# The second layer's feed-forward as one part of 448 columns, with other cuts of the kept V and of w2

## The chip, the cores and the metric

The kernel runs on one core of a Trainium2 chip. The metric is the device time of one execution in microseconds. Three runs of the kernel before gave 707.36, 707.47 and 707.51; their median is 707.47. One execution more was recorded by the hardware profiler.

## The reference

Two identical layers of a decoder are applied to four tokens (one for each of four batch rows), x of shape [4, 512]. Each layer is attention over a cache, and then a gated feed-forward, each behind a layer normalisation and added to x:

```
x = x + attention(norm(x), k_cache, v_cache, wq, wo)
x = x + feed_forward(norm(x), w1, w3, w2)

attention:    q = x @ wq                          # 32 heads of 128; 8 key/value heads, 4 query heads each
              p = softmax(q k^T / sqrt(128))      # over 4096 cached positions
              out = (p v) @ wo
feed_forward: h = silu(x @ w1) * (x @ w3)         # 512 -> 1792
              out = h @ w2                        # 1792 -> 512
```

Both layers use the same weights and the same caches. All is f32: the K cache and the V cache hold 67 MB each, wq and wo 8.4 MB each, w1, w3 and w2 3.7 MB each.

## The kernel before, in words

The kernel is a stream of loads into one large buffer, the arena, with 216 places of 256 f32 columns on all 128 partitions (`KB = 256`). One such unit is 131 kB. A list, `plan`, names all loads in the order in which they are issued, all on SyncE's queue; `pump` issues the next load as soon as the arena has a free stretch for it, and `done` gives a load's places back when the last of its parts has been used. Nothing is scheduled by the framework: every engine works in the order of the code.

For each of the eight key/value heads a K load and a V load of 64 units each come in turn. `scores` multiplies the padded q with K into `s_ps` (32 products of 512 columns), `factors` and `exponents` make the softmax, `turn_p` transposes it, and `weigh` multiplies it with V into `o_ps`: two halves of 16 products, each followed by a scaling (on ScalarE for the first, VectorE for the second half), then four transposes. Layer 1 goes through the heads upward, layer 2 downward, so that the last V of layer 1 (head 7, `TURN`) is kept in the arena at places 128 to 191 for layer 2. It is the line `cache("v", 0, TURN, (32, 16, 8, 8))`: four loads of 32, 16, 8 and 8 units, where one tile of V (four products) takes 8 units. Behind it in the plan stand wo, and layer 1's w1, w3 and w2 in small loads.

`project_o` multiplies with wo, `collect` sums the partial rows of x and gives the normalised input, and `feed_forward` does the rest of the layer. In it the 1792 columns are spread over four groups of 32 PSUM partitions, so each group holds 448 columns (`FJ`). They are handled in two parts, 256 (`FA`) and 192 (`FB`) columns: `product` does 16 matmuls of w1 into `s_ps` (four blocks of the 512 inputs, four groups), the same for w3 into `o_ps`; `gate` is a sigmoid on ScalarE and a multiply on VectorE; `join` multiplies with the w3 side. w1 and w3 lie in memory as first all columns of part a, then all of part b, so that each part is one stretch. In layer 2 the loads are w1a and w3a (16 units each), w1b and w3b (12 units each), and w2 in five (8, 8, 8, 2, 2).

`tiles` copies the transposed h to `hT`; `tail_tiles` transposes what lies beyond column 256. In layer 2 w2's 14 row blocks are then multiplied into `x_ps` (four products of 128 columns each), on top of the residual `xt`, which four products with the identity put there. `busy(n)` issues n matmuls whose result nobody reads. At the end `x_ps` is copied and stored.

## Time and profile before

| what | value |
|---|---|
| median of 3 runs | 707.47 us (707.36 to 707.51) |
| the profiled execution | 707.43 us, its span 705.5 us |
| granted TensorE clock, mean | 0.804 of full speed |
| TensorE busy (matmul) | 397.1 us, 56% of the span |
| VectorE, ScalarE busy | 85.0 us, 38.3 us |
| read from memory | 298.85 MB, 424 GB/s over the span |
| share of the load queue in 16 DMA engines' span | 99.1% |
| loads issued by SyncE into the arena | 93 |

The page's busy shares say which engine is full; its queue lines say the same for the DMA engines. A timeline row tells when an engine's instruction began, how long it took, how long the engine stood idle before it, and whose signal ended that idle time. Where that is a DMA, the engine was ahead of the stream; where it is another engine, the stream was ahead. The profile counts each f32 matmul of the program as two records.

### The profile page before, as it was taken

What the parts mean: (1) busy time and instruction counts of PE and PEld (TensorE: products, weight loads), DVE (VectorE), ACT (ScalarE), POOL (GpSimd) and SP (SyncE); (2) the same over time, 40 slices, a digit from 0 to 9 for tenths busy, and PEclk for the clock granted to TensorE, in tenths of its full rate; (3) what the DMA queues carried; (4) which work ended last, traced back from release to release, by engine and by line L of the source; (5) the groups of instructions that cost most, each with busy time, mean ns of one, the idle gap of its engine ahead of it and who ended that gap; (6) DMA issues with size and microseconds to landing.
All of it is one profiled execution on the core that took longest, in us unless ns stands there. A gap on an engine that the chain in (4) does not pass through costs nothing. (4 is left out here: it accounts for less than half of the span.)

```text
span 705.5 us, 6894 instructions
## 1 busy us (share of the span) xinstructions
PE 397.1 (56%) x3082; PEld 132.4 (19%) x3082; DVE 85.0 (12%) x290; ACT 38.3 (5%) x87; POOL 2.9 (0%) x10
## 2 busy tenths in 40 slices
PE   4455453545565553547687894265563645477665
PEld 2112011111111110112143231021110211122224
DVE  2001010101001010101111111011000101010111
ACT  0000000000000000002001000000000000000101
POOL 0000000000000000000000000000000000000000
PEclk9866787767778777779899988777787868689899
DMA  9999999999999999999999999999999999999997
GB/s 387 461 402 472 413 424 439 438 421 427 454 420 436 438 425 435 427 426 421 415 404 390 402 438 445 435 431 425 438 436 431 436 435 425 442 410 433 422 425 289
DMA packets 13716, 299.36 MB, mean 424 GB/s; under 512 B 1655, under 2 KB 1783, under 8 KB 6007
## 3 DMA queue, kind: packets, MB, share of 16 engines
q1 hardware_dynamic: 13552, 298.92, 99.1%
q8 instruction: 24, 0.39, 0.2%
q14 instruction: 5, 0.04, 0.0%
q10 hardware_dynamic: 135, 0.01, 0.0%
HBM read 298.85 MB, written 0.07 MB: 424 GB/s over the span
## 5 line engine op out<-in xcount | busy, mean ns | idle before, releaser
L394 PE MATMUL o_ps<-arena 128*32 128x512 f32 x1024 | 145.4, 716 | 149.5 <-DMA arena<-in_v 135.8
L351 PE MATMUL s_ps<-arena,qpad 128*32 128x512 f32 x1024 | 149.1, 736 | 85.4 <-DMA arena<-in_kt 85.4
L394 PEld LDWEIGHTS o_ps<-arena 128*32 128x32 f32 x1024 | 37.0, 129 | 256.6 <-issue 222.3
L351 PEld LDWEIGHTS s_ps<-arena,qpad 128*32 128x32 f32 x1024 | 39.4, 131 | 178.1 <-issue 162.8
L403 DVE SCALAR_TENSOR_TENSOR p<-o_ps,parts,p 128x512 f32<-128x512 f32 x16 | 12.0, 750 | 269.4 <-PE o_ps L394 269.4
L358 DVE TENSOR_REDUCE top<-s_ps 128x1 f32<-128x512 f32 x16 | 11.0, 690 | 194.5 <-PE s_ps L351 194.5
L295 PE MATMUL o_ps<-arena,xpad 128*32 128x512 f32 x112 | 15.5, 680 | 11.6 <-DMA arena<-in_wq 11.6
L401 ACT ACTIVATE p<-o_ps,parts 128x512 f32<-128x512 f32 x16 | 11.0, 687 | 191.9 <-PE o_ps L394 183.5
L425 PE MATMUL x_ps<-arena,oT 128*4 128x512 f32 x104 | 15.2, 702 | 9.3 <-DMA arena<-in_wo 5.8
L382 PE MATMUL t_ps<-ident,p 128*128 128x128 f32 x64 | 11.4, 304 | 13.5 <-ACT p L376 13.5
L405 PE MATMUL t_ps<-ident,p 128*128 128x128 f32 x64 | 10.5, 287 | 14.3 <-DVE p L403 14.2
L369 ACT ACTIVATE f<-d 128x1 f32<-128x1 f32 x16 | 3.2, 203 | 257.2 <-DVE d L367 257.2
L376 ACT ACTIVATE p<-s_ps,top 128x512 f32<-128x512 f32 x16 | 10.9, 684 | 76.9 <-PE t_ps L405 76.9
L383 DVE COPY arena<-t_ps 128x512 f32<-128x512 f32 x16 | 11.1, 691 | 9.7 <-PE t_ps L382 9.7
L405 PEld LDWEIGHTS t_ps<-ident,p 128*128 128x128 f32 x64 | 6.7, 141 | 28.8 <-DVE p L403 28.8
L239 PE MATMUL m_ps<-ident,rows 128*32 128x128 f32 x70 | 11.9, 273 | 0.0
L382 PEld LDWEIGHTS t_ps<-ident,p 128*128 128x128 f32 x64 | 7.3, 150 | 22.2 <-ACT p L376 19.2
L458 PE MATMUL s_ps<-arena,xpad 128*32 128x192 f32 (+1 forms) x128 | 7.9, 359 | 3.7 <-DMA arena<-in_w 3.4
L458 PE MATMUL o_ps<-arena,xpad 128*32 128x192 f32 (+1 forms) x128 | 8.1, 360 | 3.1 <-DMA arena<-in_w 2.9
L239 PEld LDWEIGHTS m_ps<-ident,rows 128*32 128x32 f32 x70 | 7.5, 110 | 3.5
L295 PEld LDWEIGHTS o_ps<-arena,xpad 128*32 128x32 f32 x112 | 3.6, 124 | 21.0 <-DMA arena<-in_wq 12.5
L306 PE MATMUL m_ps<-scaled,p 128*128 128x4 f32 (+1 forms) x32 | 5.1, 293 | 1.9 <-DVE scaled L316 1.4
(97 smaller groups left out, 135.4 us busy)
## 6 DMA issues: line engine op xcount, KB each, us to landing
arena<-in_kt SPq DMA_DIRECT2D x4, 4096.0 KB, 19.5
arena<-in_v SPq DMA_DIRECT2D x4, 4096.0 KB, 37.6
arena<-in_kt SPq DMA_DIRECT2D x9, 1024.0 KB, 12.0
arena<-in_w SPq DMA_DIRECT2D x15, 512.0 KB, 7.7
arena<-in_wq SPq DMA_DIRECT2D x1, 7168.0 KB, 39.5
arena<-in_v SPq DMA_DIRECT2D x3, 2048.0 KB, 37.4
arena<-in_wo SPq DMA_DIRECT2D x1, 4096.0 KB, 24.2
arena<-in_kt SPq DMA_DIRECT2D x2, 2048.0 KB, 20.5
```

The source lines that it names most:

```text
L239: nc.tensor.matmul(m_ps[turn["m"] ^ 1][0:32, 384:512], rows, ident, start=True, stop=True)
L295: nc.tensor.matmul(ps[32 * k:32 * k + 32, :], xpad[:, k, lo:lo + 32], w[:, k, :], start=first, stop=last)
L351: nc.tensor.matmul(s_ps[32 * b:32 * b + 32, :], qpad[:, b, lo:lo + 32], k[:, j, :], start=(blk == 0), stop=(blk == NB - 1))
L358: nc.vector.tensor_reduce(top[:, 0:1], s_ps, axis=AX.X, op=ALU.max, negate=True)
L382: nc.tensor.transpose(t_ps[:, i, :], p[:, i * P:(i + 1) * P], ident)
L383: nc.vector.tensor_copy(pT.rearrange("p i r -> p (i r)"), t_ps.rearrange("p i r -> p (i r)"))
L394: nc.tensor.matmul(o_ps[32 * b:32 * b + 32, :], pT[:, i, 32 * b:32 * b + 32], w[:, b, :], start=(i == 0), stop=(i == NI - 1))
L401: nc.scalar.activation(p, o_ps, AF.Copy, scale=st["parts"][:, 0:1])
L403: nc.vector.scalar_tensor_tensor(p, o_ps, st["parts"][:, 1:2], p, op0=ALU.mult, op1=ALU.add)
L405: nc.tensor.transpose(t_ps[:, j, :], p[:, j * P:(j + 1) * P], ident)
L425: nc.tensor.matmul(x_ps[r:r + B, :], left(2 * i + n), w(n), start=first, stop=False)
L458: nc.tensor.matmul(ps[32 * j:32 * j + 32, lo:lo + n], x32[:, k, :], w[:, j * n:(j + 1) * n], start=(k == 0), stop=(k == KC - 1))
```

## The change

The plan is cut differently in three places, and layer 2's feed-forward is written in another order.

- The kept V of layer 1 comes in two loads of 32 units.
- Two more arrays are handed to the kernel: w1f and w3f hold w1 and w3 with all 448 columns of each group together. Layer 2 reads w1f in one load of 28 units, and w3f in two of 14.
- w2 in layer 2 comes in six loads (8, 8, 4, 4, 2, 2).
- Layer 2's `product` covers 448 columns for w1 and then for w3, with one `gate` in between. The residual's addition and its four products, and the four fillers, stand between the gate and w3's product; before, the fillers stood behind w1's second part and the residual behind w3's. Two joins (256 and 192 columns) follow w3, then the transposes of the first 256 columns. Layer 2 no longer runs the `Exp` on one element that stood behind its second gate. Layer 1's feed-forward is as it was.

```diff
-    cache("v", 0, TURN, (32, 16, 8, 8))
+    cache("v", 0, TURN, (32, 32))
...
-    middle(1, (16,), (12,))
-    weights("w2", w2, 1, (8, 8, 8, 2, 2), 2)
+    weights("w1", w1f, 1, (28,), 7)
+    weights("w3", w3f, 1, (14, 14), 7)
+    weights("w2", w2, 1, (8, 8, 4, 4, 2, 2), 2)
...
+        def head_tiles():
+            for i in range(2):
+                nc.tensor.transpose(t_ps[:, i, :], h[:, i * P:(i + 1) * P], ident)
+            tiles(0, 8)
+
         sq = squares()
-        product("w1a", s_ps, 0, FA, False)
+        product("w1a" if keep else "w1", s_ps, 0, FA if keep else FJ, False)
         rstd = deviation(sq, total(flat(sq)))
         mean()
-        product("w3a", o_ps, 0, FA)
-        gate(0, FA)
-        join(0, FA)
-        product("w1b", s_ps, FA, FB)
-        if not keep:
-            busy(4)
-        gate(FA, FB)
-        nc.scalar.activation(spare, half, AF.Exp)
-        for i in range(2):
-            nc.tensor.transpose(t_ps[:, i, :], h[:, i * P:(i + 1) * P], ident)
-        tiles(0, 8)
-        product("w3b", o_ps, FA, FB)
-        join(FA, FB)
-        if layer == LAYERS - 1:
+        if keep:
...
+        else:
+            gate(0, FJ)
             nc.vector.tensor_tensor(xt, xc, mu.unsqueeze(1).broadcast_to([P, KC, B]), op=ALU.add)
             for k in range(KC):
                 nc.tensor.matmul(x_ps[32 * k:32 * k + B, 0:P], xt[:, k, :], ident, start=True, stop=False)
+            busy(4)
+            product("w3", o_ps, 0, FJ)
+            join(0, FA)
+            join(FA, FB)
+            head_tiles()
...
+        "w1f": lay(w1.reshape(KC, P, 4 * FJ).transpose(1, 0, 2)).reshape(P, KC * 4 * FJ),
+        "w3f": lay(w3.reshape(KC, P, 4 * FJ).transpose(1, 0, 2)).reshape(P, KC * 4 * FJ),
```

TensorE in layer 2's feed-forward, before (line, operation, output and inputs, shape; L458 is w1's and w3's product, L246 and L287 the normalisation's sums, L239 the fillers, L489 to L501 transposes, L496 the residual, L514 w2):

```order
L458 MATMUL s_ps<-arena,xpad 32x256 x16
L246 MATMUL m_ps_120<-sq,few 128x16
L287 MATMUL m_ps_121<-off,both 128x4
L458 MATMUL o_ps<-arena,xpad 32x256 x16
L458 MATMUL s_ps<-arena,xpad 32x192 x16
L239 MATMUL m_ps_120<-ident,rows 32x128 x4
L489 MATMUL t_ps<-ident,p 128x128 x2
L458 MATMUL o_ps<-arena,xpad 32x192 x16
L496 MATMUL x_ps<-ident,xt 4x128 x4
L499 MATMUL t_ps<-ident,p 128x128
L501 MATMUL t_ps<-ident,p 64x64 x2
L514 MATMUL x_ps<-arena,qT 4x128 x16
```

and the same place in the changed kernel (its lines are numbered anew: L459 the products, L500 the residual, L240 the fillers, L479 to L510 the transposes, L523 w2):

```order
L459 MATMUL s_ps<-arena,xpad 32x448 x16
L247 MATMUL m_ps_120<-sq,few 128x16
L288 MATMUL m_ps_121<-off,both 128x4
L500 MATMUL x_ps<-ident,xt 4x128 x4
L240 MATMUL m_ps_120<-ident,rows 32x128 x4
L459 MATMUL o_ps<-arena,xpad 32x448 x16
L479 MATMUL t_ps<-ident,p 128x128 x2
L508 MATMUL t_ps<-ident,p 128x128
L510 MATMUL t_ps<-ident,p 64x64 x2
L523 MATMUL x_ps<-arena,qT 4x128 x16
```

The residual's products and the fillers moved ahead of all of w3, and the first two transposes behind it; 64 products became 32 longer ones.

SyncE's loads from the last V to the end, before:

```order
L143 DMA arena<-in_v 128x8192 x3
L143 DMA arena<-in_v 128x4096 x2
L143 DMA arena<-in_w 128x4096 x2
L143 DMA arena<-in_w 128x3072 x2
L143 DMA arena<-in_w 128x2048 x3
L143 DMA arena<-in_w 128x512 x2
```

and now:

```order
L144 DMA arena<-in_v 128x8192 x3
L144 DMA arena<-in_v 128x4096 x2
L144 DMA arena<-in_w1f 128x7168
L144 DMA arena<-in_w3f 128x3584 x2
L144 DMA arena<-in_w 128x2048 x2
L144 DMA arena<-in_w 128x1024 x2
L144 DMA arena<-in_w 128x512 x2
```

w1 and w3 come as one load and two in place of four in alternation, and w2's third load is cut in two; the bytes are the same.

## The prediction

> **What bounds the kernel now.** I read the head of the page first, then its queues and the line of the chain that ended last:

> ```profile
> span 705.5 us, 6894 instructions
> PE 397.1 (56%) x3082; PEld 132.4 (19%) x3082; DVE 85.0 (12%) x290; ACT 38.3 (5%) x87; POOL 2.9 (0%) x10
> q1 hardware_dynamic: 13552, 298.92, 99.1%
> DMA 32%; PE 9%; ACT 0%; issue 0%; DVE 0%; SPq 0%; ACTq 0%; DVEq 0%
> ```

> No compute engine is busy for more than 56% of the span, while the one queue that carries the weights and caches fills the 16 DMA engines for 99.1% of it. The kernel is a stream of 298.92 MB, and it can only get faster if the stream gets shorter, is interrupted less, or if less work is left behind its last landing. So each edit is judged by these three questions.

> Next the end of the program, in the timeline (start, duration, engine, line, operation, tiles, count, and in brackets the idle time before and what ended it; a count is in hardware passes, two for each f32 matmul of the program):

> ```profile
> 675.96 1.92 PE L394 MATMUL o_ps<-arena 128*32 128x512 f32 x16 [2.85 <-DMA arena<-in_v]
> 683.29 1.93 PE L458 MATMUL s_ps<-arena,xpad 128*32 128x256 f32 x32 [0.26 <-DVE xpad L281]
> 685.16 0.39 PE L246 MATMUL m_ps<-sq,few 128*128 128x16 f32 x2
> 686.69 0.47 ACT L466 ACTIVATE p<-s_ps,rstd 128x256 f32<-128x256 f32 x1 [4.55 <-POOL rstd L259]
> 687.20 0.48 DVE L467 SCALAR_TENSOR_TENSOR p<-s_ps,rstd,p 128x256 f32<-128x256 f32 x1 [1.17 <-ACT p L466]
> 689.57 1.51 PE L458 MATMUL s_ps<-arena,xpad 128*32 128x192 f32 x32 [1.85 <-DMA arena<-in_w]
> 691.13 0.42 ACT L466 ACTIVATE p<-s_ps,rstd 128x192 f32<-128x192 f32 x1 [3.97 <-PE s_ps L458]
> 693.17 1.51 PE L458 MATMUL o_ps<-arena,xpad 128*32 128x192 f32 x32 [0.89 <-DMA arena<-in_w]
> 694.74 0.42 DVE L471 SCALAR_TENSOR_TENSOR p<-o_ps,rstd,p 128x192 f32<-128x192 f32 x1 [2.24 <-PE o_ps L458]
> 695.08 0.17 DVE L494 TENSOR_TENSOR xt<-xpad,mu 128x16 f32<-128x16 f32 x1
> 695.30 0.40 PE L496 MATMUL x_ps<-ident,xt 128*4 128x128 f32 x8 [0.62 <-DVE xt L494]
> 695.63 0.33 PE L499 MATMUL t_ps<-ident,p 128*128 128x128 f32 x1
> 696.15 1.06 PE L514 MATMUL x_ps<-arena,qT 128*4 128x128 f32 x32
> 697.02 0.82 PE L239 MATMUL m_ps<-ident,rows 128*32 128x128 f32 x6
> 698.40 1.06 PE L514 MATMUL x_ps<-arena,qT 128*4 128x128 f32 x32 [0.56 <-DMA arena<-in_w]
> 700.97 1.62 PE L514 MATMUL x_ps<-arena,qT 128*4 128x128 f32 x48 [0.88 <-DMA arena<-in_w]
> 702.66 0.29 DVE L570 COPY p<-x_ps 128x128 f32<-128x128 f32 x1 [6.21 <-PE x_ps L514]
> ```

> Four of the waits in brackets are for weights: TensorE (PE) is ahead of the stream by 1.85 us at w1's second part, 0.89 us at w3's, 0.56 and 0.88 us at pieces of w2. PE's weight loads show the last one:

> ```profile
> 702.19 0.11 PEld L514 LDWEIGHTS x_ps<-arena,qT 128*4 128x4 f32 x8 [0.23 <-DMA arena<-in_w]
> ```

> The last eight weight loads began at 702.19 when the last piece of w2 had landed, though the 40 records before them had started at 700.97. So the end is: last landing, then 0.5 us of PE, the copy and the store. Whatever happens before 702.19 is hidden as long as PE is ready for that piece. The profiled execution took 707.43 us, 1.9 us more than its span; the median of the runs is 707.47. I add to 707.43.

> **The change, part by part.** The unit of the loads is 128 x 256 f32 (131 kB).

> Fewer loads. What does a load cost in itself? These rows show loads of 4 units, of 8 units and of 64 units arriving back to back:

> ```profile
> 376.88 0.61 PE L418 MATMUL x_ps<-arena,qT 128*4 128x256 f32 x8 [0.46 <-DMA arena<-in_w]
> 378.14 0.61 PE L418 MATMUL x_ps<-arena,qT 128*4 128x256 f32 x8 [0.45 <-DMA arena<-in_w]
> 400.84 1.06 PE L351 MATMUL s_ps<-arena,qpad 128*32 128x512 f32 x8 [0.42 <-DMA arena<-in_kt]
> 403.31 1.07 PE L351 MATMUL s_ps<-arena,qpad 128*32 128x512 f32 x8 [1.41 <-DMA arena<-in_kt]
> 578.64 5.44 PE L394 MATMUL o_ps<-arena 128*32 128x512 f32 x32 [9.34 <-DMA arena<-in_v]
> 617.35 3.64 PE L394 MATMUL o_ps<-arena 128*32 128x512 f32 x16 [9.92 <-DMA arena<-in_v]
> ```

> 4 units take 1.26 us, 8 units 2.47, and 128 units (a K and a V) 38.71, or 0.3024 a unit. At that pace 4 units are 1.21 and 8 are 2.42, so a load costs 0.05 us beyond its bytes, whatever its size. The kept V goes from four loads to two, layer 2's w1 and w3 from four to three, w2 from five to six: two loads fewer, 0.10 us. The bounds are 0 (the cost may hide in another engine's lag) and 0.2 (twice the reading). I take 0.1 off.

> Kept V in two loads. Its second half (32 units) now counts as landed only as a whole, where three landings let PE start early:

> ```profile
> 333.91 3.64 PE L394 MATMUL o_ps<-arena 128*32 128x512 f32 x32 [1.18 <-ACT p L401]
> 344.93 1.89 PE L425 MATMUL x_ps<-arena,oT 128*4 128x512 f32 x8 [5.77 <-DMA arena<-in_wo]
> ```

> wo's first 32 units follow V in the queue and were there at 344.93, so V was complete 32 x 0.3024 = 9.7 us earlier, at 335.2. PE starts its second half at 335.2 instead of 333.91, 1.3 us later. Behind it on PE is only wo's product, which waited 5.77 us for wo. The delay eats 1.3 of these 5.77, and even a half-speed pass (3.6 us more) would leave something. In layer 2 the kept V's places are given back in the same two halves, since the next K load wants 32 units at once. Cost: nothing; without the cover 1.3 us.

> One part of 448 columns. From 675.96 (last V there) to 693.17 (w3 there) 56 units came, 0.307 us each. So w1 (28 units) is complete at 684.56, w3's halves at 688.87 and 693.17. PE wants w1 at 683.29 and now waits 1.27 us. The 16 products took 1.51 us at 192 columns and 1.93 at 256, 0.0066 a column, so 3.19 at 448: PE is done with w1 at 687.75. From L246's start to the sigmoid's were 1.53 us (685.16 to 686.69), so the sigmoid starts at 689.22. Over 448 columns it takes 0.47 + 192 x 0.00078 = 0.62 and the multiply after it 0.48 + 0.18 = 0.66, so xt starts near 690.46 and the residual's products on PE 0.22 later (as 695.08 to 695.30), at 690.68.

> This is the added wait: the residual's products and four fillers now stand ahead of w3 on PE, and wait for the gate's multiply. PE is idle from 688.3 to 690.7, though half of w3 is there at 688.87. Then 0.33 us of residual, 0.97 of fillers, and w3 from 691.98 to 695.17 at PE's pace; w3's second half, there at 693.17, would have allowed 694.9. Before, w3 ended at 694.68: 0.5 us later now. Behind it came 1.47 us to w2's first product (694.68 to 696.15): join, residual, transposes. Now it is two joins (0.40 to the second, then 0.42) and the transposes, one of them moved here, about 1.45. So w2 starts at 696.6 instead of 696.15. What is late next? One piece and its fillers take 1.67 us on PE (696.15 to 697.84 with the last filler's drain), so the second piece's products can start at 698.3, where its landing allowed 698.40, and PE is free for the third at 700.0 and through its first half at 700.4; the second half lands at 700.8. So 0.4 us of cover is left at the end of the chain, and the split third piece is what makes it so: its first half is done before the second is there. The last landing still ends the program. Cost: 0.

> Sum: 707.43 - 0.1 = 707.3.

> **The clock, where this can break.** Windows of 3.41 us, laid on the steps of the granted clock (PE busy us first, PEclk third from the end):

> ```profile
> 425.32:428.73 3.41, 1.34 (x14) 0.69 (x6) 2.22 (x9) 0.87 (x3) 0.00 (x0) 1.00 0.94 404
> 428.73:432.14 3.41, 0.00 (x0) 0.00 (x0) 0.50 (x2) 0.00 (x0) 0.00 (x0) 0.50 0.98 423
> 527.72:531.13 3.41, 1.45 (x16) 0.25 (x8) 1.51 (x5) 0.15 (x1) 0.00 (x0) 1.00 1.07 461
> 531.13:534.54 3.41, 0.00 (x0) 0.00 (x0) 0.23 (x1) 0.05 (x1) 0.00 (x0) 1.00 1.02 442
> 636.94:640.36 3.42, 3.42 (x20) 1.09 (x16) 0.00 (x0) 0.00 (x0) 0.00 (x0) 0.50 1.02 441
> 640.36:643.77 3.41, 3.41 (x36) 1.26 (x32) 0.00 (x0) 0.00 (x0) 0.00 (x0) 1.00 1.00 432
> ```

> A window in which PE was busy for 1.34 us was followed by half clock, one with 1.45 was not; a full window at half clock brought full clock back. The new idle time of 2.4 us leaves at most 1.0 us of work in a window that holds all of it. Continuing the steps, 688.14 to 691.56 is such a window: half clock from 691.56 to 694.97, 1.7 us of work lost, w3 done at 696.9, w2 begun at 698.3. From there PE alone sets the pace: two pieces with fillers 3.34, then 24 products in 1.31 and a drain, 703.05 instead of 702.63. That is 707.43 + 0.42 = 707.85.

> [...]

> **The rivals.**
> 1. One cold window, as worked out: 707.85. For it: the position of the steps in this trace. Against it: where a step falls inside the gap, neither window is idle enough. It leaves the time within 0.2%.
> 2. Slower: two cold windows. The chain now has three idle times close together: 2.85 us before the last V half, 1.27 before w1, 2.4 before w3. If the steps lie so that the clock drops before w1 as well, w1 runs at half clock for a window (1.7 us late, 689.4), the gap moves with it, w3 starts at 693.7 and runs cold again to 698.6, w2 starts at 700.1, and all of w2 (4.65 us and its drain) is behind it: 705.0 to 705.4, 2.4 to 2.8 us late, so 709.8 to 710.2. It decides once both drop, that is over 0.4 + 1.7 us of delay. Against it: it takes a narrow position of the steps, about one in six by the same rows, and the time is a median of several runs.
> 3. Faster: the 16 engines finish closer together. The stream thins out at the end:

> ```profile
> 698.00:700.00 2.00, 1.60 (x38) 1.41 (x38) 0.00 (x0) 0.00 (x0) 0.00 (x0) 1.00 0.75 299
> 700.00:702.00 2.00, 1.12 (x41) 1.01 (x40) 0.00 (x0) 0.00 (x0) 0.00 (x0) 1.00 0.30 104
> ```

> In these 4 us the engines were busy (DMA share, second from the end) for 2 x 0.75 + 2 x 0.30 = 2.1 us, so an even finish would come 1.9 us sooner: 705.4. Fewer and longer loads might go some way, to 706.3 at half. Against it: the byte count of each engine is unchanged and w2's pieces are smaller.

> **How the numbers follow.** A measurement of this kernel tells about 0.2% (1.4 us) from no change, so faster means under 706.05 and slower over 708.89. Forecast 707.3 with 0.50, one cold window 0.30, two cold windows 0.11, an even finish 0.09. The first two are no change (0.80), and so is about half of the last (0.04); a fifth of rival 2 stays under the bound by its smaller prices (0.02). That gives 0.86 within, 0.09 slower, 0.05 faster. The range runs from half the even finish (706.5) to past one cold window, half way to two (708.8).

> **What would show it.** Right: PE's w1 product waits for w1 by about 1.3 us; the residual's products wait for xt and w3 starts near 692 with no DMA wait; w2 starts 0.5 us or more later; the last weight loads are still released by w2; the kept V's second half starts at 335 with wo's wait shortened by about 1.3. Half clock at 692 to 695 with PE unbroken to the end would be rival 1. Wrong: the last w2 piece lands over 1 us from 702.1, or a changed wait shows before 670 outside the kept V.

## The result, and the profile after

The changed kernel took 708.99 us (median of 22 runs, 706.98 to 713.2), the kernel before beside it on the same chip 707.42 (22 runs, 706.56 to 709.45). The ratio on record is 1.0030 with a 95% interval of [1.0018, 1.0042], slower by 0.3%; the two medians alone differ by 0.2%. The forecast was 707.3 and "no change"; the time lies 0.2 us above the range (706.5 to 708.8) and just past the bound for slower (708.89).

More telling than the median is the spread. With a second set of the same kernel (below) there are 33 runs: 14 lie under 708.9, 7 between 709 and 711, and 12 above 711. Of the kernel before beside these two sets, 54 of 57 runs lie under 709. So the change did not make every execution a little longer. It made many of them 2 to 6 us longer. The kernel before is not quite free of such runs: of 151 runs of it in all, 3 took more than 711 (up to 713.35). None of these three was profiled.

The profiled execution took 707.74 us, which is one of the better ones. The head of its page, with the load queue's line and the chain of waits by engine:

```profile
span 706.0 us, 6757 instructions
PE 399.2 (57%) x3018; PEld 131.4 (19%) x3018; DVE 84.7 (12%) x289; ACT 36.5 (5%) x84; POOL 2.9 (0%) x10
q1 hardware_dynamic: 13264, 298.92, 99.0%
DMA 31%; PE 10%; DVE 0%; issue 0%; ACT 0%; POOLq 0%
```

The stream is as it was: the same bytes, 99.0% of the span. PE's share of the chain rose from 9 to 10% and SyncE's queue left it. The kept V did what was worked out:

```profile
335.33 3.64 PE L395 MATMUL o_ps<-arena 128*32 128x512 f32 x32 [1.20 <-ACT p L402]
344.97 1.89 PE L426 MATMUL x_ps<-arena,oT 128*4 128x512 f32 x8 [4.41 <-DMA arena<-in_wo]
```

Its second half starts at 335.33 instead of 333.91, and wo's wait shrinks from 5.77 to 4.41. wo's product starts where it did. The end of the program, in the timeline (columns as before):

```profile
675.78 1.92 PE L395 MATMUL o_ps<-arena 128*32 128x512 f32 x16 [2.82 <-DMA arena<-in_v]
684.38 4.77 PE L459 MATMUL s_ps<-arena,xpad 128*32 128x448 f32 x32 [1.53 <-DMA arena<-in_w1f]
690.61 0.63 ACT L467 ACTIVATE p<-s_ps,rstd 128x448 f32<-128x448 f32 x1 [8.66 <-POOL rstd L260]
692.10 0.40 PE L500 MATMUL x_ps<-ident,xt 128*4 128x128 f32 x8 [2.40 <-DVE xt L498]
693.19 3.17 PE L459 MATMUL o_ps<-arena,xpad 128*32 128x448 f32 x29
697.46 0.19 DVE L475 COPY qT<-t_ps 128x32 f32<-128x32 f32 x1 [0.20 <-PE t_ps L479]
697.71 0.33 PE L508 MATMUL t_ps<-ident,p 128*128 128x128 f32 x1 [0.28 <-DVE qT L475]
698.23 1.06 PE L523 MATMUL x_ps<-arena,qT 128*4 128x128 f32 x32
701.18 1.58 PE L523 MATMUL x_ps<-arena,qT 128*4 128x128 f32 x45
702.85 0.29 DVE L579 COPY p<-x_ps 128x128 f32<-128x128 f32 x1 [4.32 <-PE x_ps L523]
```

Both new waits are there in about the forecast size: 1.53 us before w1 (1.27 worked out) and 2.40 before the residual (2.4). But w1 took 4.77 us, not 3.19, and from 692.10 to the end no row of PE names a DMA: w2 begins at 698.23 and PE no longer waits for it. Nor do PE's weight loads, the last 48 of which run without a break from 701.07, so the forecast's sign that w2 still releases the last ones did not come. The windows, laid on the steps of the granted clock (PE busy us first, with its records; PEclk third from the end), of the kernel before:

```profile
681.32:684.73 3.41, 2.78 (x38) 2.17 (x42) 0.81 (x5) 0.47 (x2) 0.00 (x0) 1.00 0.97 413
684.73:688.14 3.41, 2.97 (x48) 1.47 (x39) 1.23 (x6) 0.47 (x1) 0.55 (x1) 1.00 1.03 436
688.14:691.56 3.42, 1.99 (x39) 1.93 (x40) 0.14 (x1) 0.42 (x1) 0.00 (x0) 1.00 0.97 407
```

and of the changed kernel:

```profile
677.34:680.75 3.41, 1.88 (x24) 0.74 (x20) 1.22 (x3) 0.00 (x0) 0.00 (x0) 1.00 0.96 412
680.75:684.17 3.42, 1.54 (x14) 1.25 (x10) 0.94 (x5) 0.47 (x2) 0.00 (x0) 1.00 0.96 407
684.17:687.58 3.41, 3.19 (x20) 1.12 (x24) 0.00 (x0) 0.00 (x0) 0.00 (x0) 0.50 1.02 433
687.58:690.99 3.41, 2.11 (x23) 0.79 (x12) 0.40 (x4) 0.38 (x1) 0.55 (x1) 1.00 0.99 419
```

The window of `collect`, 680.75 to 684.17, held 1.54 us of PE work and was followed by half clock. Before, the same stretch held 2.78 us, since w1's first part began at 683.29 inside it. Now PE waits there for the whole of w1. (The steps of the two executions lie 0.57 us apart, so the stretches are not quite the same.) So this is the forecast's rival 1, one cold window, but the clock fell one wait earlier than it was expected to. The question for the experiments was whether the clock also makes the long executions.

### The profile page after: what moved, and what is told of

Its sections match the earlier page's. It is cut to its first block, busy times and chain, and to the rows that moved or that the text cites. A ratio compares the mean times of both kernels' runs of the same rounds, so it can differ in the third digit from the quotient of the medians.

```text
span 706.0 us, 6757 instructions
## 1 busy us (share of the span) xinstructions
PE 399.2 (57%) x3018; PEld 131.4 (19%) x3018; DVE 84.7 (12%) x289; ACT 36.5 (5%) x84; POOL 2.9 (0%) x10
## 3 DMA queue, kind: packets, MB, share of 16 engines
q1 hardware_dynamic: 13264, 298.92, 99.0%
## 5 line engine op out<-in xcount | busy, mean ns | idle before, releaser
L395 PE MATMUL o_ps<-arena 128*32 128x512 f32 x1024 | 146.9, 723 | 149.9 <-DMA arena<-in_v 135.1
L240 PE MATMUL m_ps<-ident,rows 128*32 128x128 f32 x70 | 11.9, 273 | 0.0
L459 PE MATMUL s_ps<-arena,xpad 128*32 128x256 f32 (+2 forms) x96 | 9.2, 495 | 3.1 <-DMA arena<-in_w 1.5
L459 PE MATMUL o_ps<-arena,xpad 128*32 128x256 f32 (+2 forms) x96 | 8.1, 424 | 2.1 <-DMA arena<-in_w 2.0
L240 PEld LDWEIGHTS m_ps<-ident,rows 128*32 128x32 f32 x70 | 7.5, 110 | 3.5
```

Source lines behind the costliest of these rows:

```text
L240: nc.tensor.matmul(m_ps[turn["m"] ^ 1][0:32, 384:512], rows, ident, start=True, stop=True)
L395: nc.tensor.matmul(o_ps[32 * b:32 * b + 32, :], pT[:, i, 32 * b:32 * b + 32], w[:, b, :], start=(i == 0), stop=(i == NI - 1))
L459: nc.tensor.matmul(ps[32 * j:32 * j + 32, lo:lo + n], x32[:, k, :], w[:, j * n:(j + 1) * n], start=(k == 0), stop=(k == KC - 1))
```

## The experiments

**Which part of the change costs the time.** Three kernels, each with a part of it. V only:

```diff
-    cache("v", 0, TURN, (32, 16, 8, 8))
+    cache("v", 0, TURN, (32, 32))
```

> The kernel before with the kept V in two loads, nothing else. Clock theory (the time was lost to half-clock windows of TensorE in layer 2's feed-forward) and stream theory (w1 and w3 in the new layout, in long loads, come slower or uneven) both expect no loss here: 707.3, that is 0.1 us under before for two loads fewer, highest run not above before's. A theory that the kept V's later start costs time expects 708 to 709.

Measured: 707.48 (12 runs, 707.03 to 708.84) against 707.61; ratio 0.9994 [0.9985, 1.0003]. w2 only:

```diff
-    weights("w2", w2, 1, (8, 8, 8, 2, 2), 2)
+    weights("w2", w2, 1, (8, 8, 4, 4, 2, 2), 2)
```

> The kernel before with w2 in six loads, nothing else. All theories that put the loss in the feed-forward's first half expect 707.4 to 707.5 (one load more, 0.05 us); if the smaller last loads were the cause, 708 to 709.

Measured: 707.61 (706.8 to 709.49) against 707.61; ratio 1.0002 [0.9992, 1.0011]. The feed-forward only, that is the changed kernel with V and w2 as before:

```diff
-    cache("v", 0, TURN, (32, 32))
+    cache("v", 0, TURN, (32, 16, 8, 8))
...
-    weights("w2", w2, 1, (8, 8, 4, 4, 2, 2), 2)
+    weights("w2", w2, 1, (8, 8, 8, 2, 2), 2)
```

> The new feed-forward and the new layout of w1 and w3, but the kept V in four loads and w2 in five as before. Clock theory and stream theory: the whole loss is here, median 708.5 to 709.5, single runs up to 712 or 713, and at least 3 us between the runs. If the loss needs the kept V or w2's cut, 707.5 with runs within 1.5 us.

Measured: 710.55 (707.97 to 713.61, four of 12 above 711) against 707.61; ratio 1.0038 [1.0023, 1.0052]. The two other parts do nothing that can be measured; all of the loss is in the feed-forward, whose median lies a microsecond above the range expected.

The profiled execution of V only is the longest of its 12 (708.84) and shows that the order of the kernel before can bear much of this. Half clock began in the wait for the last V and lasted four windows; the window that lost it, and the first and the last of the four:

```profile
674.48:677.89 3.41, 0.88 (x8) 0.29 (x12) 0.00 (x0) 0.00 (x0) 0.00 (x0) 1.00 1.00 418
677.89:681.31 3.42, 2.50 (x15) 0.76 (x8) 0.75 (x1) 0.00 (x0) 0.00 (x0) 0.50 1.01 431
688.13:691.55 3.42, 3.42 (x35) 1.47 (x23) 0.00 (x0) 0.00 (x0) 0.00 (x0) 0.50 0.99 417
```

Yet w2 began at 699.51 there. Two executions of the changed kernel with three cold windows, of which one is shown further below, began it at 701.61 and 701.97.

**Is it the clock?** `busy(n)` gives PE products that nobody reads. In front of a wait they change no order. First in both new waits:

```diff
         sq = squares()
+        if not keep:
+            busy(5)
         product("w1a" if keep else "w1", s_ps, 0, FA if keep else FJ, False)
...
+            busy(10)
             gate(0, FJ)
```

> The changed kernel with five fillers on TensorE before w1's product (1.2 us, the wait for w1) and ten more before the residual's products (2.4 us, the wait for xt); the waits themselves stay. Clock theory: median 707.2 to 707.6, no run above 709. Stream theory and a theory by which the order alone (w3 held behind the residual) costs the time: 709 as the changed kernel, with runs up to 712, or later still by what the fillers add.

Measured: 708.03 (707.12 to 714.15) against 707.61; ratio 1.0017 [1.0000, 1.0034]. Ten of the 12 runs are under 708.8, but two are at 711.6 and 714.15, where none was expected above 709. The profiled execution was the one of 711.6, and its windows tell where that came from:

```profile
674.01:677.43 3.42, 1.10 (x12) 0.42 (x16) 0.00 (x0) 0.00 (x0) 0.00 (x0) 1.00 1.06 449
677.43:680.84 3.41, 2.49 (x12) 0.72 (x4) 0.75 (x1) 0.00 (x0) 0.00 (x0) 0.50 0.93 399
680.84:684.25 3.41, 2.26 (x18) 0.63 (x18) 0.90 (x4) 0.25 (x1) 0.00 (x0) 0.50 0.98 416
684.25:687.67 3.42, 3.42 (x17) 3.16 (x18) 0.50 (x3) 0.23 (x2) 0.00 (x0) 0.50 1.02 432
687.67:691.08 3.41, 3.41 (x24) 2.00 (x26) 0.00 (x0) 0.00 (x0) 0.00 (x0) 0.50 0.97 411
```

The clock fell in the wait for the last V (1.10 us of work), which stands in both kernels, and did not come back for four windows. PE was at work for 2.49 and 2.26 us of the first two, and that did not raise the clock; nor, here, did the third, which was full.

Then each filler alone, and the changed kernel again beside them:

> The changed kernel once more, beside the next three on one chip: 708 to 710 with runs from 707 to 713.

Measured: 710.38 (median of 11 runs, 707.89 to 713.64; a twelfth took 1198.51 us, for a reason that is not known, and is left out) against 707.58; ratio 1.0031 [1.0010, 1.0051]. This time the profiled execution took 709.15:

```profile
681.27:684.68 3.41, 1.81 (x18) 1.38 (x21) 0.51 (x3) 0.25 (x2) 0.00 (x0) 1.00 0.93 395
684.68:688.10 3.42, 3.42 (x24) 1.35 (x20) 0.00 (x0) 0.00 (x0) 0.00 (x0) 0.50 1.06 449
688.10:691.51 3.41, 1.36 (x13) 0.52 (x4) 0.86 (x5) 0.64 (x1) 0.55 (x1) 1.00 0.97 407
691.51:694.92 3.41, 3.05 (x24) 2.27 (x28) 0.30 (x2) 0.00 (x0) 0.00 (x0) 0.50 1.00 414
```

Two windows lost the clock, `collect`'s (1.81 us) and the residual's (1.36 us), and w1 and then w3 ran cold. That is the mechanism of rival 2 of the prediction, which gave 709.8 to 710.2 for it.

The filler before w1 alone, `busy(5)`:

> The changed kernel with the five fillers before w1's product only. Clock theory: the clock is kept for w1, and the wait for xt can still cost one window of half clock: 707.3 to 707.9, highest under 710. If the fillers do nothing: 709, up to 713.

Measured: 709.05 (708.24 to 712.78) against 707.58; ratio 1.0021 [1.0004, 1.0039]. A miss: it was to remove most of the loss. The profiled execution (708.66) shows why. Two of its windows, in order of time:

```profile
678.71:682.12 3.41, 2.25 (x27) 1.29 (x25) 1.06 (x5) 0.48 (x2) 0.00 (x0) 1.00 0.94 404
682.12:685.53 3.41, 3.41 (x21) 2.72 (x24) 0.34 (x2) 0.00 (x0) 0.00 (x0) 0.50 0.99 420
```

The window ended before the fillers came, at 682.71. It was lost with 2.25 us of PE work in it, far above the 1.34 to 1.45 from which the prediction had judged. The residual's wait, with no filler, then lost the clock once more. The filler before the residual alone, `busy(10)`:

> The changed kernel with the ten fillers before the residual's products only. Clock theory: w1 can still run at half clock, and then the fillers take twice their time and stand in front of w3: median 708 to 709.5, highest 711 or more. If only the wait for xt matters: 707.3.

Measured: 708.76 (707.76 to 711.45) against 707.58; ratio 1.0013 [0.9998, 1.0029]. As expected, and its profile has w1 cold (4.91 us) and w3 warm: one filler mends one of the two windows. By the times alone the two single fillers can't be told from each other, nor this one from the kernel before.

**All three waits filled.** To the two fillers comes one in the wait for the last V, where the long execution above had begun:

```diff
                 w = loaded(*key).rearrange("p (b n) -> p b n", b=B)
+                if layer and g == 0 and f == 1 and i == 2:
+                    busy(10)
```

> The changed kernel with fillers in all three idle times: ten before the second half of the last V's products (the 2.8 us wait for the last V load), five before w1, ten before the residual. The order of the work is unchanged, w3 is still held behind the residual. Clock theory: no cold window can start in this stretch, median 707.3 to 707.9, no run above 709. Order theory without the clock: the tail as in the changed kernel, 709 to 710.5 with runs over 711.

Measured: 707.77 (11 runs, 707.23 to 708.58) against 707.77; ratio 1.0001 [0.9992, 1.0009]. The order of the work is that of the changed kernel, with both joins, the residual and all transposes where the change put them, and the loss is gone, median and spread. The loads are as the change put them too, so neither these nor the order make the loss by themselves: with the waits filled there is none. So the clock is needed for it. Even so the highest of these runs, which is the profiled one, had one cold window:

```profile
681.75:685.16 3.41, 2.25 (x22) 1.98 (x26) 0.51 (x3) 0.06 (x1) 0.00 (x0) 1.00 0.95 404
685.16:688.58 3.42, 3.42 (x20) 1.17 (x23) 0.00 (x0) 0.00 (x0) 0.00 (x0) 0.50 1.00 423
```

The same filler in the kernel before:

> The kernel before with ten fillers in the wait for the last V load, nothing else. Clock theory: the kernel before loses little to cold windows there, since it has slack behind them: median 707.3 to 707.6, its highest runs (709 and more) gone. If the clock plays no part before: unchanged 707.5, 706.8 to 709.7.

Measured: 707.44 (11 runs, 706.61 to 708.75) against 707.77; ratio 0.9996 [0.9987, 1.0004]. It gives nothing that can be measured; the kernel before had no run above 708.77 beside it, so there was little to gain. Its profiled execution (707.0) shows a cold window that costs nothing in this order:

```profile
679.63:683.04 3.41, 2.57 (x30) 1.73 (x34) 0.94 (x5) 0.47 (x2) 0.00 (x0) 1.00 1.00 424
683.04:686.45 3.41, 3.41 (x33) 1.41 (x25) 0.00 (x0) 0.00 (x0) 0.00 (x0) 0.50 1.00 423
```

The first part of w1 took 3.52 us in it instead of 1.93, and w2 began at 695.77, no later than in the kernel before.

**Or is it the order?** The rival theory: the residual's products in front of w3 hold PE back, and the clock matters only because nothing is left to absorb it. Moved behind w3:

```diff
-            for k in range(KC):
-                nc.tensor.matmul(x_ps[32 * k:32 * k + B, 0:P], xt[:, k, :], ident, start=True, stop=False)
-            busy(4)
             product("w3", o_ps, 0, FJ)
+            for k in range(KC):
+                nc.tensor.matmul(x_ps[32 * k:32 * k + B, 0:P], xt[:, k, :], ident, start=True, stop=False)
+            busy(4)
```

> The changed kernel with the residual's products and the four fillers behind w3's product instead of ahead of it. Order theory (w3 held behind the residual): 707.3, narrow. Clock theory: w3's first half starts on its landing, but there are idle times before w1 and between w3's halves still, so the gain is partial: 707.5 to 708.5, highest run over 709.

Measured: 707.93 (707.19 to 708.91) against 707.58; ratio 0.9999 [0.9983, 1.0014]. From the timeline of its profiled execution (707.5):

```profile
684.84 5.51 PE L459 MATMUL s_ps<-arena,xpad 128*32 128x448 f32 x32 [1.18 <-DMA arena<-in_w1f]
690.82 1.71 PE L459 MATMUL o_ps<-arena,xpad 128*32 128x448 f32 x16
693.33 1.71 PE L459 MATMUL o_ps<-arena,xpad 128*32 128x448 f32 x16 [0.81 <-DMA arena<-in_w3f]
697.29 1.06 PE L523 MATMUL x_ps<-arena,qT 128*4 128x128 f32 x32
```

w1 ran cold for 5.51 us (half clock from 682.69 to 689.52), worse than in the changed kernel's profile, and yet w3's second half waited 0.81 us for its load. The median is the one that the clock theory expected, but no run is over 709. So both are needed for the loss: the clock takes 1.6 us or more, and the order decides whether it can be caught up. In the changed kernel PE stands still for 2.40 us behind w1 and does all of w3 afterwards. In the run above the first half of w3 was there by the time that w1 was done: its product at 690.82 names no DMA.

**Cutting w1 so that PE can begin early.** w1 in two loads, otherwise the changed kernel:

```diff
-    weights("w1", w1f, 1, (28,), 7)
+    weights("w1", w1f, 1, (14, 14), 7)
```

> The changed kernel with w1 in two loads of 14 units instead of one of 28, so that TensorE starts w1's first half at once (683.3) and has no wait of 1.3 us there. Clock theory: w1 keeps its clock more often and is done 1.4 us sooner; the wait for xt stays: 707.6 to 708.5, some runs to 711. If the wait for w1 plays no part: 709 to 710.5 as the changed kernel.

Measured: 711.49 (707.37 to 713.83; seven of 12 above 711) against 707.77; ratio 1.0042 [1.0024, 1.0060]. The largest miss of the study. Its profiled execution (707.96) kept the clock, began w1 at 682.99 and so shows nothing of the long ones. So an early start of w1 does not take the loss away. The same kernel once more:

> The kernel with w1 in two loads once more, for a profile; more than half of its runs took 711 to 714. If this one is slow, clock theory wants to see TensorE at half clock from the wait for the last V load (674 to 678) on, for three windows or more, and w3 done after 698. A slow run at full clock there would end the theory.

It took 707.68, so it is none of the long ones. It does show that `collect`'s window can be lost even when PE needn't wait for w1: the window held 2.25 us of work and ended 0.7 us before w1 began, and w1 ran cold (4.51 us). With the filler in the wait for the last V:

> The kernel with w1 in two loads (median 711.5 before) and, as its only addition, ten fillers in the wait for the last V load. If the runs of 711 to 714 begin with a cold window at that wait, they are gone: median 707.4 to 708.2, no run above 710. If they begin at the wait for xt or inside w1, they stay: median over 710.

Measured: 708.46 (707.27 to 709.55) against 707.61; ratio 1.0001 [0.9987, 1.0014]. The median is a little over the expected range. The runs above 711 are gone, so in this kernel they most likely begin at the last V; but the two sets were measured on different chips, and no long run was profiled. Seven of 12 against 12 of 33 doesn't tell whether two loads make them more frequent. That `collect`'s window is at risk even so is seen in its profile (709.55): 2.58 us of work, and half clock after it.

```profile
679.87:683.28 3.41, 2.58 (x30) 1.73 (x34) 0.94 (x5) 0.47 (x2) 0.00 (x0) 1.00 1.02 433
683.28:686.69 3.41, 3.41 (x20) 0.87 (x16) 0.00 (x0) 0.00 (x0) 0.00 (x0) 0.50 1.00 425
```

**Where the long executions begin.** Three more profiled executions of the changed kernel:

> The changed kernel once more, for a profile; about a third of its runs took 711 or more. If this one is slow: half clock from the wait for the last V load on, as above; if it is near 709: two cold windows, w1's and w3's; if near 707.7: w1's alone.

> The changed kernel once more, for a profile. If it takes 711 or more: half clock begins at the wait for the last V load (a window that ends between 676 and 680) and lasts three windows or more. At 709: two cold windows, w1's and w3's. At 707.7: w1's alone or none.

> As the run before: at 711 or more, half clock from the wait for the last V load on; at 709 w1's and w3's windows cold; at 707.7 one or none.

They took 707.98, 711.38 and 712.05 (the kernel before beside the last two 708.3). The first lost the clock in the wait for the last V, had it back before w1, and had neither w1 nor w3 cold. `collect`'s first products and w1 in the execution of 711.38, and its windows:

```profile
682.22 1.11 PE L279 MATMUL m_ps<-rows,p 128*128 128x4 f32 x8 [0.56 <-DVE p L272]
685.10 5.81 PE L460 MATMUL s_ps<-arena,xpad 128*32 128x448 f32 x32 [1.53 <-DMA arena<-in_w1f]
```

```profile
680.13:683.54 3.41, 2.37 (x26) 1.57 (x26) 0.98 (x5) 0.47 (x2) 0.00 (x0) 1.00 0.98 420
683.54:686.96 3.42, 1.89 (x13) 0.68 (x16) 0.34 (x2) 0.00 (x0) 0.00 (x0) 0.50 0.97 411
686.96:690.37 3.41, 3.41 (x24) 0.90 (x16) 0.00 (x0) 0.00 (x0) 0.00 (x0) 0.50 0.99 419
690.37:693.78 3.41, 1.07 (x12) 0.52 (x4) 1.15 (x6) 0.63 (x1) 0.55 (x1) 1.00 0.99 413
693.78:697.20 3.42, 3.35 (x27) 2.41 (x31) 0.01 (x1) 0.00 (x0) 0.00 (x0) 0.50 1.01 414
```

The two long executions did not begin at the last V, as was expected, but at `collect`. The window with `collect`'s products (2.37 us) loses the clock early, so that the wait for w1 falls into the cold window; it holds 1.89 us of work, which doesn't raise the clock, and one more cold window follows. Then the residual's wait loses it again, and w3 is cold too: three cold windows. The execution of 712.05 has the same three. What goes with it is where a step lies against `collect`'s first product: 2.09 us ahead of it here and 2.41 in the execution of 712.05, but 0.75 ahead in that of 707.74 and 0.21 behind in that of 709.15. So 1.3 us in the position of the steps go with some 4 us of time; these are four executions, not a test. A part of the two long times is not the clock's: w1 was there at 685.10 and 685.71, 0.7 and 1.3 us later than in the execution of 707.74 (684.38).

**A version without the loss.** w1 in two loads as above, and the residual's products with eight fillers between the two halves of w3, so that PE has w3's first half to do while VectorE makes xt:

```diff
...
-        def product(name, ps, lo, n, fill=keep):
+        def product(name, ps, lo, n, fill=keep, between=None):
             for k in range(KC):
+                if between and k == 2:
+                    between()
...
-            for k in range(KC):
-                nc.tensor.matmul(x_ps[32 * k:32 * k + B, 0:P], xt[:, k, :], ident, start=True, stop=False)
-            busy(4)
-            product("w3", o_ps, 0, FJ)
+            def residual():
+                for k in range(KC):
+                    nc.tensor.matmul(x_ps[32 * k:32 * k + B, 0:P], xt[:, k, :], ident, start=True, stop=False)
+                busy(8)
+
+            product("w3", o_ps, 0, FJ, between=residual)
```

> w1 in two loads, and the residual's products with eight fillers between the two halves of w3's product, where TensorE waits for w3's second load anyway. Both theories: time of the kernel before, 707.2 to 707.7, no run above 709; a version that beats the kernel before would show 0.1 to 0.2 us of gain, under what can be told apart.

Measured: 707.61 (706.64 to 710.32, four of 12 over 709, where none was expected) against 707.77; ratio 1.0008 [0.9997, 1.0019]. And with the filler in the wait for the last V on top:

> The residual's products between w3's halves, w1 in two loads, and the ten fillers in the wait for the last V load. If the runs of 709 to 710 seen without these fillers begin at that wait: median 707.1 to 707.5, no run above 708.8. If not: as without them, 707.6 with a quarter of the runs over 709.

Measured: 707.34 (706.71 to 708.67) against 707.61; ratio 0.9996 [0.9985, 1.0006]. The lowest median of all, and not to be told from the kernel before; the chip is another than in the run without the filler. In its profile w1 still ran cold, and the residual's wait was down from 2.40 to 0.38:

```profile
683.99 4.68 PE L463 MATMUL s_ps<-arena,xpad 128*32 128x448 f32 x32 [0.26 <-DVE xpad L282]
689.52 1.71 PE L463 MATMUL o_ps<-arena,xpad 128*32 128x448 f32 x16 [0.32 <-DMA arena<-in_w3f]
691.61 0.40 PE L506 MATMUL x_ps<-ident,xt 128*4 128x128 f32 x8 [0.38 <-DVE xt L502]
```

**The price of a cold window, over the runs.** The start of w2 and the span of the profiled executions (the start is that of L514, L523 or the line that answers to it):

| kernel | cold windows under w1 and w3 | w2 starts | span | from w2's start to the span's end |
|---|---|---|---|---|
| before | 0 | 696.15 | 705.5 | 9.35 |
| residual behind w3 | 2, both under w1, caught up | 697.29 | 705.7 | 8.4 |
| between the halves, filler in V | 1, under w1, caught up | 697.39 | 706.1 | 8.7 |
| changed, execution of 707.98 | 0 (last V cold) | 697.87 | 706.2 | 8.3 |
| changed | 1 | 698.23 | 706.0 | 7.8 |
| changed, again | 2 | 699.49 | 707.2 | 7.7 |
| changed, execution of 711.38 | 3 | 701.61 | 709.6 | 8.0 |

With w2 before 698 the stream sets the end, and the last column varies with it. From 698 on it is 7.7 to 8.0: PE does w2 without a pause and the span follows w2's start. The number of cold windows alone doesn't give that start: the feed-forward alone had one, under w1, and began w2 at 699.16 (span 706.8), since w1 was there only at 685.35. A median span of the kernel before is 705.6 (707.5 less 1.9), so the point from which PE decides is a start of w2 at about 697.8.

## Why the prediction was wrong, point by point

Right were the parts away from the clock, but for one term below. The kept V's delay went into wo's wait and V and w2 alone moved nothing. Both added waits on PE came in about the size worked out. The mechanism of rivals 1 and 2 is what happened, and their prices came near: one cold window had w2 at 698.3 and the last copy at 703.05, and the profile shows 698.23 and 702.85; two had w2 at 700.1 and a time of 709.8 to 710.2, and the profile shows 699.49 and 709.15. Part of that is luck. Rival 1 put the cold window on w3, and it fell on w1; it had w3 done at 696.9, which was 0.5 us too late, and the tail behind w3 0.4 us too short, so that two errors cancel. Rival 2 had all of w3 cold, 4.9 us, and it took 4.1.

**The step that failed is the clock's chances**: "a narrow position of the steps, about one in six by the same rows" for two cold windows, and the forecast of none with 0.50. The sum put the clock's cost at nothing. In 19 of 33 runs the time was 709 or more, and in 12 it was above 711. Six profiles have the feed-forward in the changed order without added fillers and with w1 in one load (the changed kernel five times, the feed-forward alone once): one has no cold window under w1 and w3, two have one, one has two and two have three. Two mistakes made the chances too kind.

First, the threshold was read from two windows alone, with 1.34 and 1.45 us of PE time. It was taken for a bound on busy time. `collect`'s windows lost the clock with 1.54, 1.81, 2.25, 2.37 and 2.58 us. They hold ten records of 4 and 16 columns (L278 and L281), which alone take 1.35 us in the execution of 707.74.

Second, the wait for w1 was costed at its 1.27 us alone, "PE is done with w1 at 687.75". The clock was examined at the residual's gap; a loss before w1 came only together with that one, in rival 2. But the first part of w1, which began at 683.29 in the kernel before, had stood in `collect`'s window. Putting 28 units into one load took that work out of the window, and the half clock then fell on w1's own product (4.77 instead of 3.19 us). That this is why the window was lost is argued and not shown. In the profile of the run with the filler before the residual, w1 began 0.26 us behind `collect`, 1.1 us of it lay in the window, and with 2.59 us of work the window was lost all the same.

**Three cold windows** were no rival at all. Half clock was priced as lasting one window. Here windows with 1.89 and 2.26 us of work stayed cold, and those with 3.05 and 3.19 brought the clock back; a cold window that begins before w1 is there isn't that full. (The full one with the two fillers stayed cold even so.)

**"About 1.45 us"** from w3's end to w2's first product is 1.87 (696.36 to 698.23). The tail's transpose L508 waits 0.28 us for VectorE's copy L475, which stands behind both joins on VectorE; the sum had left this wait out (0.28 of the 0.42). At full clock w2 would so have started at 697.0 instead of 696.6, still ahead of the 697.8 from which PE decides. This alone cost nothing, but it left 0.8 us to absorb a cold window of 1.6.

**The clock's steps.** The sum let an idle time of 2.4 us cost nothing at the clock; no run shows that its length alone makes it harmless. That of 2.40 us before the residual in the execution of 707.74 kept the clock: a step fell into it, and the windows on its two sides held 2.11 and 2.31 us of work. That of 2.41 us in the execution of 709.15 lost it, with 1.36 us in the window. The window with the idle time before w1 (1.53 us) lost it in the execution of 707.74, with 1.54 us of work. And the row of 425.32, 1.34 us of work and half clock behind it, stood beside the sum. The windows above, laid on the steps of the clock, are 3.41 or 3.42 us long, and the clock in them is 1.00 or 0.50.

**The two loads fewer** (0.10 us) can be neither confirmed nor refuted. V alone, which drops two loads, has a ratio of 0.9994 [0.9985, 1.0003]: 0.1 us is well inside that.

What stays open is what exactly the granted clock follows, where the long runs with w1 in two loads begin (with the filler in the wait for the last V there were none, but none was profiled either), what made the three long runs of the kernel before, and what sets the position of the steps against the program in an execution.

## What to carry to other kernels

A wait that is "hidden behind the stream" was not free on TensorE here: in the execution of 707.74, with 1.53 us before w1, a window of 3.41 us held 1.54 us of work, half clock followed, and w1 took 4.77 us instead of the 3.19 worked out. So see how full a wait leaves each such window, for every position of the windows, and what the next two windows then cost at half clock. When a load is made longer, ask whether the product that it feeds helped to keep the clock in the stage before; here that is a suspicion, as w1 in two loads did not take the loss away. And products that wait for another engine do not belong in front of products whose data is there: with the residual behind w3 the median was 707.93, and two cold windows under w1 were caught up.

## What the runs showed of the hardware

This goes some way with what the kernels showed: `collect`'s ten records of 4 and 16 columns keep PE busy for 1.35 us and hold 64 columns. It would also make fillers weak, as 20 records of them take 2.37 us for 2560 columns (690.58 in the run with all three waits filled), where 16 of V's take 1.92 us for 8192. But columns do not decide it alone either: two of `collect`'s windows were lost with 5184 and 5952 columns, those of 2.57 and 2.58 us above. It is a count over profiles; no run isolated it.

The way back took more. In the same two profiles the half-clock windows with up to 2.57 us of PE work (558.44 in the kernel before) were followed by half clock, 99 of them, and the 64 with 2.66 us or more by full clock. In another run even a full one was not enough, that at 684.25 with the two fillers. In between, windows neither lost the clock nor won it back: 1.99 us kept full clock at 688.14 in the kernel before, and 1.89 us left half clock at 683.54 in the execution of 711.38. One early loss lasted four windows in the profile of V only (677.89 to 691.55), and in the changed order, with TensorE busy for 57% of the span, the runs lie between 707 and 713.6 us.
